# Summing the experts' gated output in DRAM with adding DMAs from GpSimd's queue

## Chip, cores and metric

The kernel runs on one core of one Trainium2 chip. The metric is the device time of one launch in microseconds. The time before is the median of three runs, and the trace is one execution of the same program taken by the hardware profiler.

## What is computed

Three stages follow each other: a linear attention with a normalization, a feed-forward net with a leaky activation (2048 hidden columns), and a mixture of eight experts over 2304 tokens of 512 columns. The change lies in the last stage. Cut to it, the reference is:

```python
for e in range(E):                          # E = 8, w1[e] is 512 x 1024, w2[e] is 1024 x 512
    h = np.maximum(x @ w1[e], 0.0)
    ye = h @ w2[e]
    out += P[:, e:e + 1] * ye               # P: gates, tokens x experts
```

The inputs and the output are float32; `P` comes from a fixed number of row and column scalings of the exponentials of `x @ w_gate`.

## The kernel before

All products are made from halves: each float32 operand is split into two float16 parts, and three matmuls (high by high, high by low, low by high) are summed in PSUM. On top of that, both layers of an expert use a Strassen-like scheme with seven products (numbered 0 to 6) for a 2 x 2 block product. The net counts as layers e = 0 and 1 (`M` = 2), the experts as e = 2 to 9 (`NL` = 10). So "the third expert" is e = `M + 2` = 4.

The tokens are worked on in three parts p (`NP` = 3). For each expert and part there are four units of the first layer (`Quad`, matmuls of 384 columns) and then three units of the second layer (`Outs`, o = 0 to 2, matmuls of 256 columns): 9 output units for each expert. An output unit makes a 2 x 128 x 512 block of the output: two token tiles b and two column halves d, four parts c11, c12, c22 and c21. It has three chains of products on banks of PSUM:

- `chain_a` sums products 0, 5, 6 and 3 in one bank. After each of the first three, ScalarE copies the partial sum u out (`take_u`) before the next product is added. The last state is the part c21.
- `chain_c` makes product 4; VectorE adds u and has c22; product 2 is added in the same bank, and with u it is c12.
- `chain_d` makes product 1; with u it is c11.

Each of c11, c12 and c22 is then added, multiplied by the gate of its token, to a sum buffer in SBUF (`add_to`); c21 goes there directly from PSUM. There are two sum buffers (`acc`), used in turn, so unit n uses the buffer of unit n - 2. Before the adds, SP loads the sums of the former experts from `accd` in DRAM (`acc_load`); after them it stores the buffer to `accd` (`end`, `store`). The first expert (e = 2) leaves its bare product there, the second multiplies it by the first gate. The last expert stores each part to the result `out` as soon as it is there, 128 KB at a time.

What sets the order: all instructions of all engines are put in line by a planner (`Sched`) before the launch. It runs the program as a model several times, derives a latest start of each step from the run before, and always takes the step with the earliest start and then the least due time. A step with several ways (a list) is given to the engine that is free first. Each engine and each DMA queue then runs its list strictly in order. SP's queue carries the weights, the inputs x (`x_load`), and the traffic of `accd`; GpSimd's queue carries three small loads at the start. Nearly all instructions outside the matmuls are issued through one helper and show as line L164; matmuls of the products show as L403.

Of the kernel before, what the change touches and what calls it, by code (L numbers as in the profile page):

```python
# [15 lines left out]
AF = mybir.ActivationFunctionType  # L16
# [242 lines left out]
def fused_kernel(ctx: ExitStack, tc: tile.TileContext, qT, k, v, g_norm, w_in, w_out, alpha,  # L259
# [7 lines left out]
    nc = tc.nc  # L267
# [35 lines left out]
    def program(sc):  # L303
# [712 lines left out]
        def acc_load(n):  # L1016
            e, p, o = outs[n]
            if n >= 2:
                yield acc_left[outs[n - 2]]
            if e > M:  # L1020
                yield acc_left[e - 1, p, o]
                yield from dma(P * D * 8, (acc[n % 2], accd[p * TPB + o].rearrange("p (b d) -> p b d", b=2)))
            acc_ready[e, p, o].set()
# [19 lines left out]
        class Unit:  # L1043


            def __init__(self, n, turn, raw):
                self.n, self.turn, self.held, self.raw = n, turn, 2, raw
                self.buf = [raw[:, q, :] for q in range(4)]
                self.u, self.c22 = [ev() for _ in range(3)], ev()
# [231 lines left out]
        class Outs(Unit):  # L1281
# [38 lines left out]
            def end(self, b, d):  # L1320
                acc_done[self.e].set()
                self.adds -= 1
                if self.e == NL - 1:
                    t, sl = self.ts[b], slice(d * 256, (d + 1) * 256)
                    sc.add(self.store(P * D * 2, out[t * P:(t + 1) * P, sl], self.acc(b, d)))
                elif self.adds == 0:
                    sc.add(self.store(P * D * 8, accd[self.p * TPB + self.o].rearrange("p (b d) -> p b d", b=2), self.sums))

            def store(self, nbytes, dst, src):
                yield from dma(nbytes, (dst, src))  # L1330
# [31 lines left out]
            def take_c21(self, ps):  # L1362
# [5 lines left out]
                self.give(ps)  # L1368
                self.end(1, 0)

        seats = Slots(sc, range(3))

        def layers():

            todo, late, slot, users = [], [], 0, {}
            for k_, (e, p) in enumerate(order):
                net = e < M
                keys = [(b, f) for b in range(2) for f in range(8)] if net else \
                    [(m_, i) for i in range(4) for m_ in range(7)]
                for key in keys:  # L1380
                    hop_done[(e, p), *key], hop_used[(e, p), *key] = ev(), ev(DC if net else TPB)
                    hop[(e, p), *key] = hops[slot]
                    hop_free[(e, p), *key] = users[slot] if slot in users else \
                        kv_done[2 if slot < 13 else 3] if slot < 26 else spread_done
                    users[slot] = hop_used[(e, p), *key]
                    slot = (slot + 1) % len(hops)
                split = len(late) if not net else len(late) // 2 if k_ in (1, NP) else 0
                todo += late[:split] + [(Quad, e, p, i) for i in range(4)] + late[split:]
                late = [(Ys, e, p, b, o) for b in range(2) for o in range(DC)] if net else []
                if not net:  # L1390
                    todo += [(Outs, e, p, o) for o in range(TPB)]
            for n, (kind, e, p, *x) in enumerate(todo):
                if kind == Ys:
                    seat = yield from seats.get()
                    Ys(n, seat, e, p, *x).start()
                    continue
                turn = yield from flight.get()
                if kind == Quad:
                    yield xb_ready[e][p]
                    if e < M:  # L1400
                        yield const_ready
                raw = yield from unit_bufs.get()
                kind(n, turn, raw, e, p, *x).start()
# [135 lines left out]
```

## Time and profile before

| | |
|---|---|
| median of three runs | 1807.35 us |
| lowest, highest | 1801.12 us, 1809.96 us |
| profiled execution, first to last instruction | 1807.8 us |
| TensorE, VectorE, ScalarE busy | 1770.8 us, 1438.4 us, 1156.5 us |
| GpSimd busy | 5.9 us |
| moved by DMA | 195.16 MB |

The span of the profiled execution is the only time that its page gives. The busy times are averages over stages with different limits, so a stage is read from its own stretch, and what ends a wait there. A granted clock of 1.00 is 2.4 GHz, 0.50 would be 1.2 GHz.

### The profile page before, as it was taken

Reading aid. Unit: us, or ns where it says so; the run is one execution under the profiler, and the core shown is the slowest. Engines: PE = TensorE matmul, PEld = TensorE weight load, DVE = VectorE, ACT = ScalarE, POOL = GpSimd, SP = SyncE. Lnnn points to the kernel's source line nnn. Section 1 sums busy time; section 2 is a strip of 40 time slices with the busy share of each in tenths; the row PEclk is TensorE's granted clock in tenths of the full one; section 3 lists DMA queues with packets and bytes.
Section 4 is the critical chain, followed back from the end, with each engine's and each line's share of the span. In section 5 each row is a group of like instructions: output and inputs, shape, how many; then the busy total and the mean of one; then the engine's idle time right before and its main releaser. Section 6 shows DMA issues by size and latency. Waiting matters only on the chain.

```text
span 1807.8 us, 32280 instructions
## 1 busy us (share of the span) xinstructions
PE 1770.8 (98%) x12898; PEld 1277.1 (71%) x12898; DVE 1438.4 (80%) x3158; ACT 1156.5 (64%) x2463; POOL 5.9 (0%) x15
## 2 busy tenths in 40 slices
PE   4999999999999999999999999999999999999999
PEld 3765666666677767777777777777777777777777
DVE  4789976668777999899868878886998688788666
ACT  5767864636586777667746666764677576566443
POOL 1000000000000000000000000000000000000000
PEclk9789999999999999999999999999999999999999
DMA  9532221302032042513423331343224234212231
GB/s 307 176 108 106 68 71 62 108 1 108 1 143 85 24 155 94 189 53 138 161 88 117 144 123 43 130 166 127 80 108 174 71 117 148 104 36 101 102 132 47
DMA packets 52598, 195.16 MB, mean 108 GB/s; under 512 B 4944, under 2 KB 12640, under 8 KB 49760
## 3 DMA queue, kind: packets, MB, share of 16 engines
q1 hardware_dynamic: 52304, 193.09, 30.1%
q8 instruction: 100, 1.64, 0.4%
q14 instruction: 50, 0.41, 0.1%
q0 software_dynamic: 144, 0.03, 0.0%
HBM read 141.58 MB, written 51.51 MB: 107 GB/s over the span
## 4 chain that ended last, share of the span: by engine, by line
PE 93%; DVE 3%; ACT 2%; DMA 1%; issue 0%; SPq 0%; ACTq 0%
PE ps L403 89%; DVE arena L164 3%; ACT arena L164 2%; PE ps L450 2%; DMA arena<-in_v_dram 1%; PE ps L164 1%; PE ps L531 1%; PE ps L541 1%; DMA arena<-in_w_in_dram 0%; PE ps L712 0%; SPq L164 0%; PE ps L501 0%; ACT L164 0%; ACTq L164 0%
## 5 line engine op out<-in xcount | busy, mean ns | idle before, releaser
L403 PE MATMUL ps<-arena 128*128 128x256 f16 (+1 forms) x12240 | 1678.8, 300 | 7.4 <-DVE arena L164 3.8
L403 PEld LDWEIGHTS <-arena 128*128 128x128 f16 x12240 | 1196.8, 98 | 477.7 <-issue 12.4
L164 ACT ACTIVATE arena<-arena 128x384 f16<-128x384 f32 (+6 forms) x1577 | 871.4, 598 | 238.9 <-DVE arena L164 186.9
L164 DVE TENSOR_TENSOR arena<-arena 128x384 f16<-128x384 f32 (+7 forms) x1566 | 826.2, 572 | 53.1 <-ACT arena L164 47.3
L164 ACT ACTIVATE arena<-ps 128x384 f32<-128x384 f32 (+3 forms) x691 | 306.4, 452 | 352.7 <-PE ps L403 331.2
L164 DVE SCALAR_TENSOR_TENSOR arena<-arena 128x384 f32<-128x384 f32 (+3 forms) x558 | 308.5, 562 | 36.2 <-DMA arena<-accd 17.1
L164 DVE SCALAR_TENSOR_TENSOR arena<-ps,arena 128x384 f32<-128x384 f32 (+1 forms) x423 | 233.7, 555 | 79.0 <-PE ps L403 63.7
L164 DVE TENSOR_TENSOR arena<-ps,arena 128x256 f32<-128x256 f32 x216 | 90.7, 425 | 97.5 <-ACT arena L164 58.6
L164 ACT ACTIVATE arena<-ps,arena 128x384 f32<-128x384 f32 x96 | 55.4, 580 | 52.1 <-PE ps L403 50.8
L450 PE MATMUL ps<-arena 128*128 128x128 f32 (+1 forms) x160 | 37.8, 402 | 24.4 <-DMA arena<-in_v_dram 24.4
L450 PEld LDWEIGHTS ps<-arena 128*128 128x128 f32 (+1 forms) x160 | 31.6, 284 | 29.2 <-issue 28.4
L164 DVE TENSOR_SCALAR arena<-arena 128x1 int32<-128x1 int32 (+8 forms) x198 | 45.0, 242 | 8.8 <-ACT arena L164 6.7
L164 DVE SCALAR_TENSOR_TENSOR arena<-arena,ps 128x384 f32<-128x384 f32 x24 | 14.4, 613 | 28.9 <-PE ps L403 28.7
L164 DVE TENSOR_REDUCE arena<-ps 128x1 f32<-128x128 f32 x26 | 7.5, 287 | 30.9 <-PE ps L164 30.8
L164 DVE TENSOR_REDUCE arena<-arena 128x1 f32<-128x384 f32 (+7 forms) x66 | 22.5, 349 | 6.4 <-ACT arena L164 5.9
L541 PEld LDWEIGHTS ps<-arena 128*128 128x128 f32 x144 | 20.9, 219 | 4.8 <-issue 2.5
L531 PE MATMUL ps<-arena 128*128 128x384 f32 (+1 forms) x64 | 22.6, 496 | 0.0
L541 PE MATMUL ps<-arena 128*128 128x2 f32 x144 | 21.3, 270 | 0.9 <-ACT arena L164 0.9
L164 PE MATMUL ps<-arena 128*128 128x128 f32 (+2 forms) x92 | 21.2, 303 | 0.5 <-ACT arena L164 0.5
L164 ACT ACTIVATION_READ_ACCUMULATOR arena<-arena 128x1 f32 x96 | 18.5, 193 | 0.0
L164 DVE TENSOR_TENSOR arena<-arena,ps 128x384 f32<-128x384 f32 x24 | 12.7, 549 | 6.6 <-PE ps L164 6.3
L531 PEld LDWEIGHTS ps<-arena 128*128 128x128 f32 x64 | 13.2, 232 | 3.8 <-issue 2.2
(25 smaller groups left out, 50.8 us busy)
## 6 DMA issues: line engine op xcount, KB each, us to landing
arena<-xd SPq DMA_DIRECT2D x16, 2688.0 KB, 9.6
arena<-in_w_dram SPq DMA_DIRECT2D x64, 512.0 KB, 4.5
accd<-arena SPq DMA_DIRECT2D x63, 512.0 KB, 2.9
arena<-accd SPq DMA_DIRECT2D x63, 512.0 KB, 3.7
xd<-arena SPq DMA_DIRECT2D x5, 2688.0 KB, 9.7
arena<-in_w_in_dram SPq DMA_DIRECT2D x16, 512.0 KB, 5.2
arena<-in_w_out_dram SPq DMA_DIRECT2D x16, 512.0 KB, 4.5
arena<-in_qT_dram SPq DMA_DIRECT2D x6, 768.0 KB, 7.9
```

The costliest lines, as they stand in the source:

```text
L164: way[2](*way[3], **way[4])
L403: r = nc.tensor.matmul(ps[:, 0:ncols], x, y, start=(start and i == 0 and m == 0), stop=(stop and i == n - 1 and m == 2), skip_group_check= ...
L450: nc.tensor.matmul(ps[:, sl], kt[0:n, c, sl], vt[0:n, c, sl], start=(c == 0), stop=(c == 4))
L531: nc.tensor.matmul(ps[:, r0:r1], kvbd[b][:, c, :], qs[j][:, c, r0:r1], start=True, stop=True)
L541: nc.tensor.matmul(sums[:, o * H + 2 * c:o * H + 2 * c + 2], sq[:, o * P:(o + 1) * P], heads, start=True, stop=True)
```

## The change

For the experts e = 4 to 9 a new class, `Adds`, takes the place of `Outs`. Every part leaves PSUM multiplied by the gate, the three u as well as c11, c12, c22 and c21 before anything is added to them. Each of the seven drains can go to ScalarE or VectorE. The adding is left to DMA, into `out` itself: u0 and u1 (both column halves of the first tile, 256 KB) and u2 (one half of the second tile, 128 KB) by `store_first`, then the whole sum buffer (512 KB) by `store_last`, which waits until the first two have landed. These DMAs have the accumulate operation and are issued on GpSimd's queue. The sum buffers are still two, used in turn; they are no longer loaded, and a buffer is free again when the 512 KB add of its unit has landed. The second expert (e = 3) stores its sums to `out` in place of `accd`, and only it loads from `accd`.

```diff
@@ -1017,7 +1017,7 @@
             e, p, o = outs[n]
             if n >= 2:
                 yield acc_left[outs[n - 2]]
-            if e > M:
+            if e == M + 1:
                 yield acc_left[e - 1, p, o]
                 yield from dma(P * D * 8, (acc[n % 2], accd[p * TPB + o].rearrange("p (b d) -> p b d", b=2)))
             acc_ready[e, p, o].set()
@@ -1320,11 +1320,11 @@
             def end(self, b, d):
                 acc_done[self.e].set()
                 self.adds -= 1
-                if self.e == NL - 1:
-                    t, sl = self.ts[b], slice(d * 256, (d + 1) * 256)
-                    sc.add(self.store(P * D * 2, out[t * P:(t + 1) * P, sl], self.acc(b, d)))
-                elif self.adds == 0:
-                    sc.add(self.store(P * D * 8, accd[self.p * TPB + self.o].rearrange("p (b d) -> p b d", b=2), self.sums))
+                if self.adds == 0:
+                    dst = accd[self.p * TPB + self.o].rearrange("p (b d) -> p b d", b=2)
+                    if self.e > M:
+                        dst = out.rearrange("(j o p) d -> o p j d", o=TPB, p=P)[self.o][:, 2 * self.p:2 * self.p + 2, :]
+                    sc.add(self.store(P * D * 8, dst, self.sums))
 
             def store(self, nbytes, dst, src):
                 yield from dma(nbytes, (dst, src))
@@ -1367,6 +1367,71 @@
                     yield from self.add_to(1, 0, ps[:, 0:256])
                 self.give(ps)
                 self.end(1, 0)
+
+        class Adds(Outs):
+
+
+            def __init__(self, n, turn, raw, e, p, o):
+                super().__init__(n, turn, raw, e, p, o)
+                self.flat = raw.rearrange("p q n -> p (q n)")
+                self.left, self.first, self.last_, self.added = 2, ev(3), ev(4), ev()
+                self.dst = out.rearrange("(j o p) d -> o p j d", o=TPB, p=P)[o][:, 2 * p:2 * p + 2, :]
+
+            def start(self):
+                super().start()
+                sc.add(self.store_first())
+                sc.add(self.store_last())
+
+            def gated(self, dst, ps, b):
+                col = pcols[self.e % 3][:, self.ts[b]:self.ts[b] + 1]
+                return [A(256, nc.scalar.activation, dst, ps[:, 0:256], AF.Copy, scale=col),
+                        V(256, nc.vector.tensor_scalar, dst, ps[:, 0:256], col, None, op0=mult)]
+
+            def take_u(self, ps, n):
+                yield pcol_done[self.e]
+                yield self.gated(self.flat[:, n * 256:(n + 1) * 256], ps, n // 2)
+                self.u[n].set()
+                self.first.set()
+
+            def take(self, ps, b, d, after):
+                yield pcol_done[self.e]
+                yield acc_ready[self.e, self.p, self.o]
+                yield self.gated(self.acc(b, d), ps, b)
+                after()
+                acc_done[self.e].set()
+                self.last_.set()
+
+            def take_c11(self, ps):
+                return self.take(ps, 0, 0, lambda: banks.put(ps))
+
+            def take_c12(self, ps):
+                return self.take(ps, 0, 1, lambda: self.give(ps))
+
+            def take_c22(self, ps):
+                return self.take(ps, 1, 1, self.c22.set)
+
+            def take_c21(self, ps):
+                return self.take(ps, 1, 0, lambda: self.give(ps))
+
+            def add(self, nbytes, *parts):
+                for dst, src in parts:
+                    yield "G", 1.0, nc.gpsimd.dma_start, (dst, src), {"accum_op": add}
+                sc.dma_free = max(sc.dma_free, sc.now + 0.65) + nbytes / 180e3
+                yield sc.dma_free + 1.5
+
+            def store_first(self):
+                yield self.first
+                x = self.flat[:, 0:768]
+                yield from self.add(P * 256 * 12, (self.dst[:, 0, :], x[:, 0:512]), (self.dst[:, 1, 256:512], x[:, 512:768]))
+                self.added.set()
+                self.release()
+
+            def store_last(self):
+                yield self.last_
+                yield self.added
+                yield from self.add(P * D * 8, (self.dst, self.sums))
+                acc_left[self.e, self.p, self.o].set()
+                self.release()
 
         seats = Slots(sc, range(3))
 
@@ -1388,7 +1453,7 @@
                 todo += late[:split] + [(Quad, e, p, i) for i in range(4)] + late[split:]
                 late = [(Ys, e, p, b, o) for b in range(2) for o in range(DC)] if net else []
                 if not net:
-                    todo += [(Outs, e, p, o) for o in range(TPB)]
+                    todo += [(Outs if e < M + 2 else Adds, e, p, o) for o in range(TPB)]
             for n, (kind, e, p, *x) in enumerate(todo):
                 if kind == Ys:
                     seat = yield from seats.get()
```

The planner puts the whole program in line anew. GpSimd's queue, its last rows before (`arena` is SBUF, `in_...` are inputs):

```order
L1430 MEMSET arena 64x1
L1431 MEMSET arena 128x2048 [waits Pool_49]
L1433 DMA arena<-in_g_norm_dram 64x1 x2
L1434 DMA arena<-in_alpha_dram 128x16x1
L1435 DMA arena<-in_w_gate_dram 128x4x8
L1535 UNCONDITIONAL_BRANCH
L1535 ISA [waits barrier_Pool_Activation_PE_DVE_SP_gather]
```

and after, the rows of the three output units of the second part of e = 5; `out_dram` is the result, 128x512 is the DMA of u0 and u1, 128x256 that of u2, 128x2x512 that of the sum buffer; DMASW are the semaphores of DMAs from this queue:

```order
L164 DMA out_dram<-arena 128x512 [waits DVE_49,Activation_49]
L164 DMA out_dram<-arena 128x256 [waits Activation_49]
L164 DMA out_dram<-arena 128x512 [waits DVE_49,Activation_49]
L164 DMA out_dram<-arena 128x256 [waits DMASW3_49,Activation_49]
L164 DMA out_dram<-arena 128x2x512 [waits DMASW4_49,DMASW1_49,DMASW0_49]
L164 DMA out_dram<-arena 128x2x512 [waits DMASW3_49,DMASW2_49,Activation_49]
L164 DMA out_dram<-arena 128x512 [waits DVE_49,Activation_49]
L164 DMA out_dram<-arena 128x256 [waits DMASW7_49,DVE_49]
```

Where the queue ended with the start-up loads, 162 adding DMAs now stand. The two first units' 512 KB adds stand behind the small adds of the second unit and wait for DMAs of the same queue, and the third unit's small adds stand behind them.

VectorE in an output unit of e = 5 before; `ps` are banks of PSUM, DMAHW are semaphores of DMAs from SP's queue:

```order
L164 TENSOR_TENSOR arena<-ps_64,arena 128x256 [waits PE_49]
L164 SCALAR_TENSOR_TENSOR arena<-arena 128x256 [waits DMAHW1_49,DVE_49]
L164 TENSOR_TENSOR arena<-ps_66,arena 128x256 [waits Activation_49]
L164 SCALAR_TENSOR_TENSOR arena<-arena 128x256 [waits DVE_49]
L164 SCALAR_TENSOR_TENSOR arena<-ps_68,arena 128x256 [waits PE_49]
L164 TENSOR_TENSOR arena<-ps_66,arena 128x256 [waits PE_49]
```

and VectorE after, at the third of the three units named above and into the first-layer units behind it:

```order
L164 TENSOR_SCALAR arena<-ps_65,arena 128x256 [waits PE_49]
L164 TENSOR_SCALAR arena<-ps_66,arena 128x256 [waits DMASW4_49,Activation_49]
L164 TENSOR_SCALAR arena<-ps_67,arena 128x256 [waits PE_49,Activation_49]
L164 SCALAR_TENSOR_TENSOR arena<-ps_68,arena 128x384 [waits Activation_49]
L164 SCALAR_TENSOR_TENSOR arena<-ps_70,arena 128x384 [waits PE_49]
L164 SCALAR_TENSOR_TENSOR arena<-ps_68,arena 128x384 [waits PE_49]
```

and ScalarE after, at the same third unit:

```order
L164 ACTIVATE arena<-ps_65,arena 128x256 [waits PE_49]
L164 ACTIVATE arena<-ps_69 128x384 [waits DVE_49,PE_49]
L164 ACTIVATE arena<-ps_67,arena 128x256 [waits DMASW4_49,Activation_49]
L164 ACTIVATE arena<-ps_69 128x384 [waits PE_49]
L164 ACTIVATE arena<-ps_65,arena 128x256 [waits PE_49,Activation_49]
L164 ACTIVATE arena<-ps_69 128x384 [waits PE_49]
```

The sums out of PSUM and the gated adds are gone; one gated drain each stands for them, on either engine. The first drain of each engine that writes the sum buffer again waits for a semaphore of GpSimd's DMAs (DMASW4), and the drains of the first-layer units (128x384) stand behind it.

## Rows read from the trace of the kernel before

**Rows 1.** The page: busy time of each engine, and the chain's shares by engine.

```profile
PE 1770.8 (98%) x12898; PEld 1277.1 (71%) x12898; DVE 1438.4 (80%) x3158; ACT 1156.5 (64%) x2463; POOL 5.9 (0%) x15
...
PE 93%; DVE 3%; ACT 2%; DMA 1%; issue 0%; SPq 0%; ACTq 0%
```

**Rows 2.** Busy time in stretches: start:end, length, engines busy (instructions), clock, DMA share, GB/s.

```profile
40.00:145.00 105.00, 103.64 (x536) 72.31 (x535) 82.46 (x213) 75.96 (x171) 0.00 (x0) 0.82 0.42 139
520.00:780.00 260.00, 253.90 (x2018) 188.35 (x2016) 225.76 (x550) 188.82 (x399) 0.00 (x0) 1.00 0.30 113
780.00:845.00 65.00, 64.45 (x493) 48.02 (x492) 60.57 (x136) 49.67 (x106) 0.00 (x0) 1.00 0.27 92
880.00:1700.00 820.00, 819.71 (x6289) 615.51 (x6288) 655.90 (x1392) 521.16 (x1130) 0.00 (x0) 1.00 0.31 111
1205.00:1370.00 165.00, 165.00 (x1267) 123.85 (x1266) 134.39 (x282) 108.38 (x236) 0.00 (x0) 1.00 0.31 111
```

**Rows 3.** The chain in order of time: start, length, what, instructions.

```profile
510.30 7.20 PE ps L403 x66
...
590.80 12.69 PE ps L403 x78
...
824.95 12.96 ACT arena L164 x27
...
1531.09 269.49 PE ps L403 x2064
```

**Rows 4.** The timeline of the last 8 us: start, length, engine, what, [idle before].

```profile
1801.04 2.91 PE L403 MATMUL ps<-arena 128*128 128x256 f16 x24 [0.47 <-ACT arena L164]
...
1804.51 0.48 DVE L164 SCALAR_TENSOR_TENSOR arena<-arena 128x256 f32<-128x256 f32 x1
```

**Rows 5.** Groups by shape: count, busy us, mean ns, idle before.

```profile
L164 ACT ACTIVATE arena<-ps 128x384 f32<-128x384 f32 x456 | 219.5, 488 | 140.9 <-PE ps L403 131.8 <-PE ps L531 5.2 <-PE ps L541 1.7
...
L164 DVE TENSOR_TENSOR arena<-ps,arena 128x256 f32<-128x256 f32 x216 | 90.7, 425 | 97.5 <-ACT arena L164 58.6 <-PE ps L403 37.8
L164 DVE SCALAR_TENSOR_TENSOR arena<-arena 128x256 f32<-128x256 f32 x189 | 89.5, 485 | 19.5 <-DMA arena<-accd 17.1 <-DMA out_dram<-arena 0.3
L164 ACT ACTIVATE arena<-ps 128x256 f32<-128x256 f32 x225 | 84.4, 381 | 200.5 <-PE ps L403 199.4
...
L164 ACT ACTIVATE arena<-ps,arena 128x384 f32<-128x384 f32 x96 | 55.4, 580 | 52.1 <-PE ps L403 50.8 <-DVE arena L164 0.4
...
L164 DVE SCALAR_TENSOR_TENSOR arena<-ps,arena 128x256 f32<-128x256 f32 x63 | 30.6, 485 | 35.0 <-PE ps L403 35.0
...
L164 DVE TENSOR_SCALAR arena<-arena 128x256 f32<-128x256 f32 x36 | 12.0, 354 | 0.4 <-DMA arena<-accd 0.3
```

**Rows 6.** SP's own waits: total us, times, longest.

```profile
SPq L164 <- DVE arena L164: 1135.1, 148, 64.0
```

**Rows 7.** Waits of the engines: total us, times, longest.

```profile
DVE arena L164 <- DMA arena<-accd: 17.4, 11, 3.7
```

**Rows 8.** GpSimd's timeline at the start: its DMA instructions.

```profile
4.67 1.19 POOL L1434 DMA_DIRECT2D arena<-in_alpha_dram  x1
5.85 0.77 POOL L1435 DMA_DIRECT2D arena<-in_w_gate_dram  x1
```

**Rows 9.** DMA issues: instructions, KB each, median us from issue to landing.

```profile
arena<-xd SPq DMA_DIRECT2D x16, 2688.0 KB, 9.6
...
accd<-arena SPq DMA_DIRECT2D x63, 512.0 KB, 2.9
arena<-accd SPq DMA_DIRECT2D x63, 512.0 KB, 3.7
...
out_dram<-arena SPq DMA_DIRECT2D x36, 128.0 KB, 1.8
...
arena<-in_g_norm_dram POOLq DMA_DIRECT2D x2, 0.2 KB, 6.0
arena<-in_alpha_dram POOLq DMA_DIRECT2D x1, 8.0 KB, 8.8
```

## The prediction, made before the changed kernel ran

> **What bounds the kernel now.** I read the shares first. TensorE is busy for 98% of the span, VectorE 80%, ScalarE 64%, GpSimd for nothing after the start [rows 1]. A share is no proof that TensorE has nothing to give, so I went to the stretches. From 880 us to 1700 us, five expert lengths, TensorE is busy for all but 0.3 of 820 us at a granted clock of 1.00 (2.4 GHz) [rows 2]. The chain of waits, in order of time, has one piece of 269.49 us with 2064 matmuls without a break, up to 1800.6 us [rows 3]. The last question is whether the matmuls inside are at their own pace. 66 matmuls of 256 columns take 7.20 us, 109 ns each, and 78 of 384 columns take 12.69 us, 163 ns each [rows 3]. One expert has 504 of the wide and 756 of the narrow kind: 504 x 0.163 + 756 x 0.109 = 164.6 us, and a stretch of 165 us holds 1267 matmuls [rows 2]. So TensorE's own rate is the bound wherever the changed units run, and drains and DMA lie beside it.
>
> The Trainium skill, "TensorE: Matmul & The Clock Gate", section on 56 against 53.3 ns, gives 2.5 ns over columns divided by 2.4 GHz for a matmul in a dense run. The trace agrees (109 ns for 256 columns). By it an expert cannot take under 164.3 us, which speaks against any gain from faster drains.
>
> Where TensorE does wait is earlier: 6.1 us in 520 to 780, 0.55 us in 780 to 845 [rows 2]. The six changed experts end with the last matmul at 1803.95 us [rows 4]; at 165 us each they begin near 814 us. TensorE's idle time that the changed units could win back is therefore about 1 us: 0.29 us in the steady stretch, the 0.55 us at 780 to 845 and the 0.47 us before the last 24 matmuls [rows 2, 4].
>
> **The change, part by part.** Each expert has 9 output units, so 54 units change, in 18 groups of three; 0.109 us is the price of a narrow matmul throughout.
>
> Arithmetic. Away go, per unit, three sums out of PSUM (0.425 us), three gated adds (0.485 us) and one gated add out of PSUM (0.485 us) on VectorE, 3.2 us, and three copies of 0.381 us on ScalarE [rows 5]. For 54 units that is 173 us of VectorE and 62 us of ScalarE. Seven gated drains per unit come in, 378; the order puts 299 on ScalarE and 79 on VectorE. No row has one. On ScalarE, a 384-column drain costs 0.488 us plain and 0.580 us with a scale column [rows 5], so I take 0.381 + 0.092 = 0.47 us; on VectorE 0.42 us, between the 0.354 us tensor_scalar in SBUF and the 0.425 us sum from PSUM. ScalarE gains 299 x 0.47 - 62 = 79 us, VectorE loses 173 - 79 x 0.42 = 140 us; in an expert's 165 us ScalarE goes from 108 to 121 us and VectorE from 134 to 111 [rows 2]. Neither becomes the bound, and TensorE does not run faster for it. Price: 0.
>
> SP. 54 loads and 54 stores of accd (9 of these come back as stores to the result) and the 36 small stores of the result go. SP now stands for 1135 us waiting for VectorE [rows 6], mostly in stores, with the weight and x loads behind; those loads can now start earlier. VectorE's 17.4 us of waits for accd [rows 7] shrink too. The chain is 93% TensorE and 1% DMA [rows 1]; from 825 to 838 us it runs through ScalarE [rows 3], before the first changed drains (814 us plus four first-layer units of 27 us in all), and after that nearly always through TensorE. Price: 0.
>
> GpSimd's adds. This is the unknown. Each unit issues three adding DMAs (256 KB, 128 KB, then 512 KB), and the last waits for the other two. No row shows an adding DMA. Issue: two that GpSimd does issue take 1.19 and 0.77 us of its time [rows 8]; I take 0.77 us. Landing L of 512 KB: from below, a plain store of that size, 2.9 us; from above, the slowest DMA from GpSimd's queue, 8.8 us, which ran while the start-up loads filled the engines [rows 9]. Between: stores of 128 and 512 KB land in 1.8 and 2.9 us, so 1.4 us plus 0.37 us per 128 KB; loads of 512 and 2688 KB in 3.7 and 9.6 us, so 2.3 us plus 1.4 us per 512 KB. An add must read the destination and the source before it writes. A load and a store end to end give 3.7 + 2.9 = 6.6 us; both reads pipelined, one fixed part of 2.5 us (my choice, a load's 2.3 and a little) plus 2 x 1.4 us, give 5.3 us. I take 5.3 us, since in every row bytes stream through the engines rather than in phases; the first pair then takes L1 = 3.9 us. The ends stay 2.9 (L1 2.2) and 8.8 us (L1 6.0, as the g_norm loads) [rows 9].
>
> The Trainium skill, "DMA: Bandwidth & Descriptors", section on the GpSimd path, gives 2.0 us plus bytes over 436 GB/s; "Collectives: The Full Stack", section on the bandwidth ceiling, says an add in the DMA engine halves the rate because it reads two sources. Together an estimate of 4.4 us (L1 3.2). No run here shows it; by it the sum below would be 1.6 us lower and the verdict the same.
>
> Who waits for an add: a sum buffer is used again two units later, so only the third unit of a group follows closely; before the next group stand four first-layer units, 168 wide matmuls, 27 us. The third unit's first gated drain waits for the first unit's 512 KB add, and in the queues of ScalarE or VectorE everything behind it waits as well. I counted matmuls in the new order from the one that feeds the first unit's third u part to the first that needs the third unit's drained part: 130 to 152 in 17 groups, 14.7 to 18.1 us at the two prices (the last group has no such matmul). What has to fit: drain 0.47 + two issues 1.54 + L1 3.9 + issue 0.77 + L 5.3 + drain 0.47 = 12.5 us. It fits in all, with 2 us over in the tightest. End to end (L1 5.1, L 6.6) it is 15.0 us: over in one group, by 0.3 us. At the upper end it is 18.1 us: over in 16 of 17, 25 us in all. **Price taken: 0; bounds 0 and 25 us.** Other transfers can stretch an add: an x load of 2688 KB, 9.6 us [rows 9], starts as each group begins. The margin of 2 us covers that only in part; I put 1 us for a few collisions.
>
> End. Now the last matmul ends at 1803.95 us, two VectorE steps and a 128 KB store follow, and the span ends at 1807.8 us (the table of times): 3.85 us [rows 4, 9]. In the new order the last unit's third u part is fed 18 matmuls, 2.0 us, before the end; then 0.47 + 1.54 + 3.9 + 0.77 + 5.3 = 12.0 us, so the end is 10.0 us after the last matmul: **+6.1 us**. With the lower bound +2.0, end to end +8.6, with the upper +11.7 us.
>
> Before the third expert. Nothing is added there, but the planner orders the whole program by one set of due times, and the order already differs in the first 45 matmul rows. In those stretches TensorE waits 1.4 us (40 to 145 us) and those 6.1 us [rows 2]; I allow 3 us either way and take 0.
>
> Sum: 6 + 1 + 0 = +7 us on the profiled 1807.8 us, 1814.8 us; that span lies 0.45 us above the median of the three runs, so 1814 us, 0.4% over the median.
>
> **The rivals.** First, the adds land too late and hold the drains of the third unit: a wait for a DMA in place of one for arithmetic. Against it: 2 us of margin at the value taken. For it: no row shows an adding DMA, and all of GpSimd's landed slowly. It decides once L1 + L passes about 11.5 us; at the upper end +25 and +11.7 give 1844 us, and each further us of L + L1 costs about 17 us. Slower; 0.25. Second, the relief of VectorE and SP pays: the waits of 520 to 845 us go with the new order, 6.6 us, and the adds land as fast as stores, +2 us: 1803 us. For it: those waits are put down to VectorE and ScalarE; against it: no unit before 814 us loses an instruction. 0.08. Third, the planner's new order before 814 us is itself worse by up to 6 us: 1820 us; 0.10. That the change does not do what it says I give nothing: the new order shows all 162 adds and all 378 gated drains.
>
> **How the numbers follow.** The forecast, hidden adds and a longer end, has 0.57: 1809 to 1817 us. The measurement tells about 0.5% from no change, 9 us: 1798.3 to 1816.4 us. Of the forecast's 0.57 about 0.13 lies above (L over 6.5 us); with the first rival's 0.22 and the third's 0.07 slower has 0.42. Faster by over 0.5% needs more than all waits of TensorE after 500 us: 0.02. Same: 0.56. The range 1802 to 1842 us reaches to the second rival and most of the first; at most 0.2 lie beyond.
>
> **What would show it.** Right: TensorE still busy for 165 of 165 us in the steady stretches, ScalarE near 121 and VectorE near 111 us there; 512 KB adds that land in 4 to 7 us; no waits of ScalarE or VectorE for an adding DMA that reach TensorE; some 10 us between the last matmul and the end. Wrong: TensorE idle before narrow matmuls once per group, ended by ScalarE or VectorE and behind them a DMA to the output; adds over 8 us; or a difference that is there before 814 us.

## The result and the profile after

The changed kernel takes 1819.52 us (median of 20 runs, 1812.04 to 1826.62) and the kernel before 1808.19 us (20 runs). The ratio is **1.0066, 95% interval 1.0053 to 1.0080**: slower by 12 us (9.6 to 14.5). The 20 runs of either kernel fall into 7 shorter and 13 longer ones, and the changed kernel is 11.5 us slower among the shorter and 12.1 us among the longer, so the 12 us are not a matter of the mix. The profiled execution has a span of 1818.2 us, 10.4 us over that of before.

The page, busy time of each engine and the last chain's shares by engine; these answer to [rows 1]:

```profile
PE 1770.1 (97%) x12898; PEld 1274.8 (70%) x12898; DVE 1324.0 (73%) x2859; ACT 1227.3 (67%) x2600; POOL 166.2 (9%) x177
...
PE 83%; DVE 8%; ACT 4%; DMA 3%; issue 1%; SPq 0%; POOLq 0%; ACTq 0%
```

VectorE has 114 us less to do and ScalarE 71 us more, and TensorE's busy time is what it was. The time went elsewhere. The same stretches as in [rows 2] (start:end, length, busy time and instructions of TensorE, its weight loads, VectorE, ScalarE and GpSimd, then clock, DMA share, GB/s):

```profile
40.00:145.00 105.00, 103.99 (x542) 72.43 (x541) 81.36 (x209) 76.89 (x174) 0.00 (x0) 0.82 0.44 145
520.00:780.00 260.00, 252.25 (x1994) 187.06 (x1993) 223.49 (x542) 187.19 (x395) 0.00 (x0) 0.99 0.31 112
780.00:845.00 65.00, 64.72 (x488) 47.58 (x486) 59.90 (x134) 49.53 (x108) 0.00 (x0) 1.00 0.21 70
880.00:1700.00 820.00, 818.41 (x6268) 613.22 (x6266) 565.17 (x1151) 580.11 (x1241) 132.39 (x135) 1.00 0.51 104
1205.00:1370.00 165.00, 164.49 (x1259) 122.94 (x1257) 116.54 (x237) 120.58 (x257) 26.73 (x27) 1.00 0.51 110
```

In 880 to 1700 us TensorE is idle for 1.6 us, against 0.3 us before; in 520 to 780 for 7.8 us, against 6.1 us. The end is the largest single piece. The timeline of the last 15 us (start, length, engine, what, [idle before]):

```profile
1804.29 4.16 PE L403 MATMUL ps<-arena 128*128 128x256 f16 x36 [0.23 <-ACT arena L164]
...
1804.54 0.90 POOL L164 DMA_DIRECT2D out_dram<-arena  x1 [3.45 <-ACT arena L164]
1806.45 0.47 ACT L164 ACTIVATE arena<-ps,arena 128x256 f32<-128x256 f32 x1 [1.85 <-PE ps L403]
...
1807.22 0.86 POOL L164 DMA_DIRECT2D out_dram<-arena  x1 [1.78 <-ACT arena L164]
1808.55 0.47 ACT L164 ACTIVATE arena<-ps,arena 128x256 f32<-128x256 f32 x1 [0.90 <-PE ps L403]
1810.70 1.20 POOL L164 DMA_DIRECT2D out_dram<-arena  x1 [2.62 <-DMA out_dram<-arena]
```

The last matmul ends at 1804.29 + 4.16 = 1808.45 us and the last drain at 1809.02 us. GpSimd then sits until 1810.70 us, waiting for the small add that it issued at 1807.22 us, and only then issues the last 512 KB. The span ends at 1818.2 us, **9.75 us after the last matmul; before it was 3.85 us** [rows 4].

The adding DMAs and the plain ones beside them (issues, KB each, median us from the start of the issue to the landing; [rows 9]):

```profile
out_dram<-arena POOLq DMA_DIRECT2D x54, 512.0 KB, 6.2
out_dram<-arena POOLq DMA_DIRECT2D x54, 256.0 KB, 4.5
...
out_dram<-arena POOLq DMA_DIRECT2D x54, 128.0 KB, 3.2
...
accd<-arena SPq DMA_DIRECT2D x9, 512.0 KB, 2.6
```

The groups by shape that came in (count, busy us, mean ns, idle before and what ended it; [rows 5]): the adds' issue on GpSimd, and the gated drains on ScalarE and VectorE.

```profile
L164 POOL DMA_DIRECT2D out_dram<-arena x162 | 160.3, 1052 | 1644.9 <-DVE arena L164 1044.2 <-ACT arena L164 537.5 <-DMA out_dram<-arena 33.9
...
L164 ACT ACTIVATE arena<-ps,arena 128x256 f32<-128x256 f32 x299 | 134.3, 472 | 160.8 <-PE ps L403 154.0 <-DMA out_dram<-arena 5.2
...
L164 DVE TENSOR_SCALAR arena<-ps,arena 128x256 f32<-128x256 f32 x79 | 37.2, 481 | 178.5 <-PE ps L403 157.4 <-DMA out_dram<-arena 20.5
```

The waits (total us, times, longest): the drains do wait for adding DMAs, 11 times and 25.7 us in all, up to 8.3 us at once; TensorE's own waits for the two engines, before the matmuls of line L403, are 10.0 us in all.

```profile
POOL out_dram L164 <- DMA out_dram<-arena: 33.9, 13, 5.7
...
DVE arena L164 <- DMA out_dram<-arena: 20.5, 7, 8.3
...
PE ps L403 <- ACT arena L164: 5.7, 9, 1.7
...
ACT arena L164 <- DMA out_dram<-arena: 5.2, 4, 3.2
PE ps L403 <- DVE arena L164: 4.3, 5, 2.6
```

### The profile page after: what moved, and what is told of

It reads as the page before. It is cut to its first block, busy times and chain, and to the rows that moved or that the text cites. A ratio compares the mean times of both kernels' runs of the same rounds, so it can differ in the third digit from the quotient of the medians.

```text
span 1818.2 us, 32451 instructions
## 1 busy us (share of the span) xinstructions
PE 1770.1 (97%) x12898; PEld 1274.8 (70%) x12898; DVE 1324.0 (73%) x2859; ACT 1227.3 (67%) x2600; POOL 166.2 (9%) x177
## 4 chain that ended last, share of the span: by engine, by line
PE 83%; DVE 8%; ACT 4%; DMA 3%; issue 1%; SPq 0%; POOLq 0%; ACTq 0%
PE ps L403 80%; DVE arena L164 8%; ACT arena L164 4%; PE ps L450 1%; DMA arena<-in_v_dram 1%; DMA arena<-in_w_dram 1%; PE ps L531 1%; PE ps L164 1%; PE ps L541 1%; DMA arena<-in_w_in_dram 1%; SPq L164 0%; DMA arena<-accd 0%; DMA out_dram<-arena 0%; PE ps L712 0%; PE ps L501 0%
## 5 line engine op out<-in xcount | busy, mean ns | idle before, releaser
L403 PE MATMUL ps<-arena 128*128 128x384 f16 (+1 forms) x12240 | 1681.2, 300 | 10.4 <-ACT arena L164 5.7
L403 PEld LDWEIGHTS <-arena 128*128 128x128 f16 x12240 | 1197.3, 98 | 483.7 <-issue 16.2
L164 ACT ACTIVATE arena<-ps 128x384 f32<-128x384 f32 (+3 forms) x529 | 247.3, 475 | 158.5 <-PE ps L403 137.0
L164 ACT ACTIVATE arena<-ps,arena 128x256 f32<-128x256 f32 (+1 forms) x395 | 189.9, 498 | 214.8 <-PE ps L403 206.8
L164 POOL DMA_DIRECT2D out_dram<-arena x162 | 160.3, 1052 | 1644.9 <-DVE arena L164 1044.2
L164 DVE SCALAR_TENSOR_TENSOR arena<-ps,arena 128x384 f32<-128x384 f32 (+1 forms) x369 | 206.9, 564 | 84.0 <-PE ps L403 57.4
L164 DVE SCALAR_TENSOR_TENSOR arena<-arena 128x384 f32<-128x384 f32 (+3 forms) x396 | 231.1, 591 | 16.5 <-ACT arena L164 13.6
L164 DVE TENSOR_SCALAR arena<-ps,arena 128x256 f32<-128x256 f32 (+1 forms) x82 | 38.2, 475 | 179.8 <-PE ps L403 157.4
L164 DVE TENSOR_TENSOR arena<-ps,arena 128x256 f32<-128x256 f32 x54 | 22.6, 420 | 14.8 <-PE ps L403 11.3
L164 DVE TENSOR_REDUCE arena<-arena 128x1 f32<-128x384 f32 (+7 forms) x66 | 22.4, 349 | 10.5 <-ACT arena L164 9.8
L541 PEld LDWEIGHTS ps<-arena 128*128 128x128 f32 x144 | 20.4, 214 | 4.5 <-issue 2.2
```

The lines of the kernel that those rows point to most:

```text
L164: way[2](*way[3], **way[4])
L403: r = nc.tensor.matmul(ps[:, 0:ncols], x, y, start=(start and i == 0 and m == 0), stop=(stop and i == n - 1 and m == 2), skip_group_check= ...
L541: nc.tensor.matmul(sums[:, o * H + 2 * c:o * H + 2 * c + 2], sq[:, o * P:(o + 1) * P], heads, start=True, stop=True)
```

## How the kernels below are compared

Executions of one and the same kernel differ by up to 19 us (before, 35 runs of one series: 1798.72 to 1817.60 us). Part of that lies in the start: from 40 to 145 us the granted clock was 0.76 to 0.89 in the profiles of this case, where later stretches, up to the last matmul, have 0.97 to 1.00. A span of a single profile therefore proves little, and each kernel below is judged by its ratio to runs of before on the same chip. Its profile gives two things that the start doesn't touch: the **end**, from the last matmul to the end of the span, and TensorE's **idle** time from 145 us to the last matmul. Against before (end 3.85 us, idle 6.64 us up to 845 us and 0.76 us after) they make a sum that can be set beside the ratio:

| kernel | end | idle 145 to 845 | idle 845 to last matmul | sum over before | ratio, as us of 1808 | ratio [95%] |
|---|---|---|---|---|---|---|
| changed | 9.75 | 8.0 | 2.3 | +8.9 | +11.9 | 1.0066 [1.0053, 1.008] |
| 1 no adds | 1.47 | 8.5 | 1.4 | +0.1 | +3.4 | 1.0019 [0.9998, 1.004] |
| 2 plain copies | 6.3 | 8.8 | 2.6 | +6.5 | +8.0 | 1.0044 [1.0019, 1.007] |
| 3 one more copy | 13.5 | 7.9 | 11.4 | +21.6 | +22.2 | 1.0123 [1.0089, 1.0156] |
| 4 two more copies | 18.1 | 8.5 | 51.8 | +67.1 | +88 | 1.0487 [1.0455, 1.052] |
| 5 last expert as before | 4.0 | 8.5 | 5.5 | +6.8 | +5.4 | 1.003 [1.0006, 1.0054] |
| 6 last expert only | 10.6 | 7.7 | 2.2 | +9.2 | +11.6 | 1.0064 [1.0039, 1.009] |
| 7 before, order 0.39 | 3.9 | 7.9 | 1.2 | +1.8 | +0.9 | 1.0005 [0.998, 1.003] |
| 8 before, order 0.41 | 3.9 | 8.0 | 2.2 | +2.9 | +1.4 | 1.0008 [0.9984, 1.0032] |
| 9 changed, order 0.39 | 9.4 | 11.3 | 3.2 | +12.6 | +13.6 | 1.0075 [1.005, 1.0101] |
| 10 changed, order 0.41 | 9.8 | 11.6 | 3.2 | +13.4 | +15.0 | 1.0083 [1.0056, 1.011] |

Kernel 4 apart, the sum stands within 3.4 us of the measured loss everywhere, which is within every interval but that of the changed kernel, where it falls 0.7 us short of the lower end. So the two terms are most of the account, and the experiments say what each is made of. Two cautions go with the columns of idle time. The changed kernel and kernels 1 to 4 have one order, and from 145 to 845 us they show 7.9 to 8.8 us, so a difference under 1 us between two profiles shows nothing. And profiles differ in how far they are at 845 us, so a wait near it can fall on either side; the two columns together are safer than each. (In kernel 4 the granted clock after 845 us is 0.98 as well; 2% of its 1024 us there is 20 us, which is about what the sum lacks.) Kernel 4 from 845 us to its last matmul:

```profile
845.00:1869.16 1024.16, 972.39 (x7319) 723.34 (x7316) 638.53 (x1302) 660.53 (x1417) 216.63 (x265) 0.98 0.61 149
```

## Experiments

**Theory:** the loss is the longer end, some 6 us, and little else; the adds fit behind the matmuls. **First rival:** the adds hold the drains of the third unit of each group. **Second rival:** the planner's new order is what costs.

### Kernels 1 and 2: no adds, and copies in place of adds

Both keep the changed kernel's order on every engine.

```diff
-                    yield "G", 1.0, nc.gpsimd.dma_start, (dst, src), {"accum_op": add}
+                    yield "G", 1.0, lambda *a: None, (dst, src), {}                  # kernel 1
+                    yield "G", 1.0, nc.gpsimd.dma_start, (dst, src), {}              # kernel 2
```

> The changed kernel with every instruction of every engine in the same order, but without its 162 adding DMAs (the output then lacks the experts from the third on). Theory end (the loss is mainly the two adds in series after the last matmul): no DMA waits, last matmul some 2 to 3 us earlier than in the changed kernel, span ending within 1 us of the last drain, so about 9 us less behind the last matmul; time 1807 to 1810 us against 1819.5, ratio to the kernel before 0.999 to 1.001. Theory order (the planner's new order costs the time before the third expert): time over 1812 us, since the order is untouched. Theory hold (the adds hold the drains of the third units): as theory end, but the last matmul 5 us or more earlier than in the changed kernel.

> The changed kernel with the same order, its 162 DMAs as plain copies from the same queue in place of adds (the output is then the last product written, not the sum). It prices the adding by itself. If adding reads two sources and so takes longer, 512 KB land in 4 to 5 us against 6.2, the two in series at the end save 2 to 3.5 us, and the waits of the third units shrink: time 1815 to 1817.5 us, ratio 1.004 to 1.005. If the landing is set by GpSimd's queue and not by the adding: 512 KB still near 6 us, time as the changed kernel, ratio 1.0066.

Kernel 1's last timeline rows:

```profile
1793.17 4.16 PE L403 MATMUL ps<-arena 128*128 128x256 f16 x36 [0.23 <-ACT arena L164]
...
1797.43 0.47 ACT L164 ACTIVATE arena<-ps,arena 128x256 f32<-128x256 f32 x1 [0.90 <-PE ps L403]
```

The last drain ends the program, 1.47 us after the last matmul. The ratio falls from 1.0066 to 1.0019, by 8.5 us; the end is shorter by 9.75 - 1.47 = 8.3 us. One wait of TensorE, 0.78 us, falls just behind 845 us in the changed kernel and ahead of it in kernel 1:

```profile
845.50 1.25 PE L403 MATMUL ps<-arena 128*128 128x256 f16 x10 [0.78 <-ACT arena L164]
```

```profile
835.27 0.93 PE L403 MATMUL ps<-arena 128*128 128x256 f16 x7 [0.78 <-ACT arena L164]
```

Over both columns TensorE's idle time falls from 10.4 to 9.9 us, where before has 7.4 us. So nearly everything that the adds cost in this order is the end. By what was expected it is a miss all the same: 1812.62 us lies over the 1807 to 1810 us of the theory of the end and just over the 1812 us of the theory of the order, and 1.0019 lies over 0.999 to 1.001, though its interval reaches into that range. What stays, 1.0019, is not the adds', and by itself it isn't shown, as the interval reaches 1. Kernel 1's end is 2.4 us shorter than that of before and its idle time 2.5 us longer, so by the profile the new order and the new drains, which kernel 1 keeps, cost what the shorter end gains. Its last matmul comes 11.1 us earlier than in the changed kernel, but 10.2 of these are there at the wait shown, before any add: they come from the start of the program and not from held drains.

Kernel 2's DMAs from the same queue, same tiles, same semaphores, without the adding:

```profile
out_dram<-arena POOLq DMA_DIRECT2D x54, 512.0 KB, 3.2
out_dram<-arena POOLq DMA_DIRECT2D x54, 256.0 KB, 2.6
...
out_dram<-arena POOLq DMA_DIRECT2D x54, 128.0 KB, 2.0
```

6.2, 4.5 and 3.2 us with the adding stand against 3.2, 2.6 and 2.0 us without (expected for 512 KB were 4 to 5 us): from 128 to 512 KB an add grows by 3.0 us and a copy by 1.2 us, 2.5 times. GpSimd's issue is shorter too (in 880 to 1700 us 80.82 us for 134 DMAs, 0.60 us each, against 132.39 us for 135, 0.98 us). The end is 6.3 us, 3.5 us shorter, and the ratio 4 us lower; no wait of VectorE or ScalarE for a DMA to the result is left.

### Kernels 3 and 4: hold the sum buffer longer

Behind each 512 KB add GpSimd issues one plain copy of the sum buffer to a scratch tile (kernel 4: two), so the buffer comes free later; order otherwise as in the changed kernel.

```diff
+                def add_and_copy(dst, src):
+                    nc.gpsimd.dma_start(dst, src, accum_op=add)
+                    for _ in range(1 if src is self.sums else 0):      # kernel 4: 2
+                        nc.gpsimd.dma_start(scratch, src)
-                    yield "G", 1.0, nc.gpsimd.dma_start, (dst, src), {"accum_op": add}
+                    yield "G", 1.0, add_and_copy, (dst, src), {}
```

> The changed kernel with the same order, and behind each 512 KB add a plain 512 KB copy of the same sum buffer from the same queue to a scratch place in DRAM. The buffer is free when both have landed. Theory hold with the counted margins (14.7 to 18.1 us from the third u part to the matmul in need; chain now 0.47 + 2.1 + 4.5 + 1.05 + 6.2 + 0.47 = 14.8 us): about 1 us of issue and half a microsecond of sharing more, chain near 16 us, some 3 to 6 us in all over the 17 groups, and 1 to 2 us at the end: 1823 to 1828 us, ratio 1.008 to 1.011. If the adds had a wide margin: the end alone, 1821 us, ratio 1.0075. If the adds already held each group: 17 x 1.5 = 25 us more.

> As the run with one more copy, with two: the second waits for the first, since both write the same scratch place, so the buffer comes free about 5 us later. Theory hold with the counted margins: chain near 20 us, (20 - 16.6) us in each of 17 groups, 50 to 65 us in all, time 1870 to 1890 us, ratio 1.035 to 1.045; waits of ScalarE and VectorE for DMAs of GpSimd's queue once per group, and behind them idle time of TensorE. If the sum buffers were not the place: the time grows by the end alone, 5 to 7 us, 1826 us.

The waits of kernel 3, then those of kernel 4:

```profile
DVE arena L164 <- DMA accd<-arena: 66.8, 12, 15.7
...
PE ps L403 <- ACT arena L164: 14.3, 15, 2.3
ACT arena L164 <- DMA accd<-arena: 13.9, 6, 6.3
```

```profile
DVE arena L164 <- DMA accd<-arena: 158.6, 17, 20.4
ACT arena L164 <- DMA accd<-arena: 62.4, 15, 10.0
PE ps L403 <- ACT arena L164: 44.1, 21, 5.5
PE ps L403 <- DVE arena L164: 15.2, 9, 3.1
```

With one copy more, the drains wait in 18 places instead of 11, and TensorE's idle time after 845 us goes from 2.3 to 11.4 us; with two it goes to 51.8 us. The waits named are for the extra copies (`accd` is the scratch tile), which also lengthen GpSimd's issue and the traffic. The mechanism of the first rival is thus real, it has its place where the prediction put it, and it is steep. In the changed kernel it stands just short of its point: the drains wait already, TensorE hardly. Kernel 3's ratio, 1.0123, lies over what was expected of counted margins, but 3.8 us of it are its own longer end; kernel 4's, 1.0487, lies over 1.045.

### Kernels 5 and 6: adds everywhere but in the last expert, and only there

```diff
-                    todo += [(Outs if e < M + 2 else Adds, e, p, o) for o in range(TPB)]
+                    todo += [(Adds if M + 2 <= e < NL - 1 else Outs, e, p, o) for o in range(TPB)]   # kernel 5
+                    todo += [(Outs if e < NL - 1 else Adds, e, p, o) for o in range(TPB)]            # kernel 6
                     ...
```

In kernel 5 the last expert loads its sums from the result, as `Outs` did from `accd`, and stores its parts 128 KB at a time; in kernel 6 the experts before the last are made as before and e = 8 stores to the result. Both are planned anew.

> Experts e = 4 to 8 keep the adding DMAs; the last expert, e = 9, is made as in the kernel before (sums loaded, now from the result, added by VectorE, stored in parts of 128 KB). The planner orders the whole program anew. Theory that half of the loss is the longer end (9.75 us after the last matmul against 3.85 us): the end falls back to 3.5 to 5 us, ratio to before 1.001 to 1.005, what is left being the order's own share. Rival, that adding in DRAM holds the drains throughout: 45 of 54 units still do it, ratio 1.005 to 1.007, with waits of ScalarE and VectorE for DMAs to the result that reach TensorE.

> Only the last expert, e = 9, leaves its adding to DMAs; e = 3 to 8 load and store sums as before, and e = 8 stores its sums to the result. The planner orders the whole program anew. Theory of the longer end: the span ends 9 to 10.5 us after the last matmul, ratio to before 1.0033 (6 us) by this alone, with 3 us of order either way 1.0015 to 1.005. Rival, holds throughout: 9 of 54 units, ratio under 1.0015.

The last rows of kernel 5, then of kernel 6:

```profile
1813.42 2.91 PE L403 MATMUL ps<-arena 128*128 128x256 f16 x24 [0.47 <-ACT arena L164]
...
1816.90 0.48 DVE L164 SCALAR_TENSOR_TENSOR arena<-arena 128x256 f32<-128x256 f32 x1
```

```profile
1799.85 3.62 PE L403 MATMUL ps<-arena 128*128 128x256 f16 x31
...
1805.71 1.20 POOL L164 DMA_DIRECT2D out_dram<-arena  x1 [2.94 <-DMA out_dram<-arena]
```

Kernel 5 ends its span at 1820.3 us, 4.0 us after the last matmul; kernel 6 at 1814.1 us, 10.6 us after. Five experts of adds without the last cost 1.0030, one expert of adds at the end costs 1.0064, as much as all six. A cost that were paid in every unit would have it the other way round. That kernel 6 lies above its expected 1.005, with an end of 10.6 us just over the 10.5 us expected, may be the order's share (idle +2.4 us); another 2.4 us no stretch shows. Kernel 5 has 5.5 us idle after 845 us, more than any other kernel without extra copies. But 2.8 us of it are two waits of TensorE for ScalarE that lie ahead of its first add:

```profile
846.70 4.40 PE L403 MATMUL ps<-arena 128*128 128x384 f16 x33 [1.66 <-ACT arena L164]
852.29 2.89 PE L403 MATMUL ps<-arena 128*128 128x256 f16 x25 [1.19 <-ACT arena L164]
...
858.18 0.92 POOL L164 DMA_DIRECT2D out_dram<-arena  x1 [851.49 <-ACT arena L164]
```

So these two are not the adds' doing. Whether the adds have a part in the remaining 2.7 us (0.8 us in the kernel before) isn't shown.

### Kernels 7 to 10: the same instructions in another order

One constant of the planner is moved by 0.01, in the kernel before (7, 8) and in the changed kernel (9, 10).

```diff
-MIX = 0.4
+MIX = 0.39      # kernels 7 and 9
+MIX = 0.41      # kernels 8 and 10
```

> The kernel before with one planner constant changed (MIX 0.4 to 0.39): the same instructions, another order, no adding DMAs. Theory that a new order alone costs or gives several us: ratio away from 1 by 0.001 to 0.004, seen as TensorE's idle time between 145 and 880 us (before 6.6 us). Rival, the order is worth nothing: within 0.0007 of 1, idle time within 1 us.

> The kernel before with the same constant moved the other way (0.4 to 0.41); the order differs from TensorE's 45th row on. As for 0.39: a new order alone gives a ratio away from 1 by 0.001 to 0.004 by the one theory, within 0.0007 by the other.

> The changed kernel with the planner constant at 0.39 in place of 0.4: the same instructions in another order. Theory that the loss is the longer end (6 us) plus the waits that any new order brings (2 to 3 us of TensorE idle between 145 and 880 us) plus what the start of the program costs in this order: the end again 9.5 to 11 us after the last matmul, ratio 1.004 to 1.008. Rival, that half of the loss was bad luck of the one order: ratio 1.0035 or less, in this order or in that of 0.41.

> The changed kernel with the constant at 0.41. As for 0.39: ratio 1.004 to 1.008 with an end of 9.5 to 11 us by the one theory, 1.0035 or less by the other.

TensorE before the first changed unit, 145 to 845 us, in the kernel before, the changed one, kernel 7, kernel 8, kernel 9 and kernel 10 (columns as above; one fence each):

```profile
145.00:845.00 700.00, 693.36 (x4936) 470.07 (x4935) 576.67 (x1287) 465.19 (x962) 0.00 (x0) 1.00 0.24 87
```

```profile
145.00:845.00 700.00, 691.97 (x4912) 468.77 (x4910) 574.22 (x1281) 461.25 (x957) 0.00 (x0) 1.00 0.24 85
```

```profile
145.00:845.00 700.00, 692.06 (x4949) 471.40 (x4948) 573.84 (x1281) 465.09 (x963) 0.00 (x0) 1.00 0.25 90
```

```profile
145.00:845.00 700.00, 692.03 (x4916) 469.03 (x4914) 570.05 (x1280) 460.56 (x957) 0.00 (x0) 1.00 0.24 86
```

```profile
145.00:845.00 700.00, 688.75 (x4889) 466.51 (x4887) 570.20 (x1272) 458.30 (x950) 0.00 (x0) 1.00 0.23 84
```

```profile
145.00:845.00 700.00, 688.38 (x4898) 467.33 (x4897) 567.50 (x1269) 458.68 (x952) 0.00 (x0) 1.00 0.24 88
```

Eight orders of this program were profiled, counting kernels 5 and 6: 6.6 us idle in this stretch in the one of before, 7.7 to 8.8 us in five others, 11.3 and 11.6 us in the last two. The order of before waits least, and any other waits 1 to 5 us longer, without an instruction being added here. For the kernel before, that is too little for its ratio (1.0005 and 1.0008, and both intervals contain 1), so between the theories of kernels 7 and 8 the runs don't decide; the idle time was above the 1 us of the rival. For the changed kernel they do decide: in two other orders it is slower again, 1.0075 and 1.0083, with both intervals wholly above 1.0035 and ends of 9.4 and 9.8 us; the idle time ahead of the changed units grew by nearly 5 us, more than the 2 to 3 us expected. The loss is not bad luck of one order.

## Why the prediction was right, and where it was short

The time lies in the range, 5.5 us over the 1814 us forecast, and the mechanism is the one taken: hidden adds, a longer end. But the loss is over 0.5%, the case to which the prediction gave 0.42 and not the 0.56 of no change. By its steps:

- **TensorE is the bound, relief of VectorE and SP is worth nothing: right.** 1770.8 us busy before, 1770.1 after; VectorE 134 to 117 us and ScalarE 108 to 121 us of 165 (predicted 111 and 121). The prediction's least time of an expert, 164.3 us, should read 164.4 us, which changes nothing. VectorE's gated drain took 0.481 us, not 0.42; ScalarE's 0.472, as taken. SP waits 967.3 us for VectorE in place of 1135.1 [rows 6], and nothing came of it.

```profile
SPq L164 <- DVE arena L164: 967.3, 86, 69.3
```

- **The end, +6.1 us: right in sum, by two errors that cancel, which is luck.** Measured +5.9. From the start of the third u part's drain (1806.45 us) to the 512 KB add's issue 5.9 us were predicted, 4.25 us passed: the add of u0 and u1 was out at 1804.54 us, so one small add stood in the way and not two. From there to the end 6.1 us were predicted, 7.5 us passed. The add itself took what was taken for its issue and landing together, 0.77 + 5.3 us; it landed 6.1 us after its issue began (the view of the last add below). The other 1.4 us lie between the landing and the end of the program. The prediction's sum stops at the landing, while the 3.85 us of before, from which it is subtracted, hold such a piece: the last store, issued at 1805.0 us, landed 1.7 us later, 1.1 us before the end. Kernel 1 shows that this term is nearly the adds' whole price, and kernels 5 and 6 agree.

```profile
DMA to landing us min/median/max: 6.1/6.1/6.1
```

- **Landing, 5.3 and 3.9 us taken, with 0.77 us for each issue on top: right in sum, not as counted.** The medians of 6.2 and 4.5 us begin with the issue and hold it. The end shows this: the last small add is issued at 1807.22 us for 0.86 us, and the add that waits for it starts at 1810.70 us, 3.5 us after the issue's start and 2.6 us after its end, where the median of that size is 3.2 us. So 0.77 + 5.3 = 6.1 us and 0.77 + 3.9 = 4.7 us are what to set against 6.2 and 4.5 us; GpSimd's issue alone was longer, 1.05 us. Whether the two reads are pipelined, as taken, isn't shown by this. The estimate of 4.4 us that the prediction drew from the Trainium skill ("DMA: Bandwidth & Descriptors", section on the GpSimd path, with "Collectives: The Full Stack", section on the bandwidth ceiling) is further off. The plain DMAs of kernel 2 agree with the first page's 2.0 us plus bytes over 436 GB/s at 512 and 256 KB (3.2 and 2.6 us), but 128 KB took 2.0 us and not 2.3, and the adding cost 2.5 times per byte and not twice.
- **The hold of the third unit, price 0 and 1 us for collisions: right in the price, with less room than thought.** The chain that had to fit, from the third u part's drain of the first unit through its 512 KB add to one more drain, was summed to 12.5 us. In the trace of the changed kernel it takes 11.0 to 16.2 us in the 17 groups, median 14.3, against the counted gaps of 14.7 to 18.1 us. The small adds took less than summed: in every group the 128 KB add was the later of the two to land, so one of them stood in the way and not both. The last link took more: the first unit's 512 KB adds, which run beside other transfers, landed after 5.9 to 11.1 us, median 7.7, and the third units', with no other add under way, after 5.6 to 6.2 us. What stretches the first ones, other adds or loads, isn't shown. So the drains wait (11 times), and yet TensorE loses about 0.5 us by the adds (10.4 us idle after 145 us, 9.9 us in kernel 1), which is within the scatter. Kernels 3 and 4 show what lies behind the edge. The longest of the 17 chains runs from the second of the two drains in the first row, on ScalarE, to the drain on VectorE that waits for the add:

```profile
1021.33 0.84 ACT L164 ACTIVATE arena<-ps,arena 128x256 f32<-128x256 f32 x2 [1.06 <-PE ps L403]
...
1037.42 0.88 DVE L164 TENSOR_SCALAR arena<-ps,arena 128x256 f32<-128x256 f32 x2 [0.82 <-DMA out_dram<-arena]
```

- **The order before the third expert, 3 us either way and 0 taken: this is the short step.** Kernel 1, without any add, has 2.5 us more idle time than before (9.9 against 7.4 us); with the adds' 0.5 us and the end's 5.9 us that makes the +8.9 us. The third rival, a worse order for up to 6 us, is therefore part of what happened, on top of the forecast and not in place of it: 2.5 us by the idle time, up to 5.5 us if the 3 us below are the order's as well; kernels 9 and 10 pay nearly 5 us there. A new order should have had a positive price, since before's order waits less than any other that was profiled.
- **What is left:** the profiled pair differs by 10.4 us, 1.5 us more than the sum, the ratio by 11.9 us (9.6 to 14.5). The sum is also short of the ratio in kernels 1 and 6, by 3.3 and 2.4 us, and over it in kernels 5, 7 and 8, by 0.9 to 1.5 us. Whether the changed order also costs something in the first 145 us, where one profile per kernel says little, stays open.

The second rival (the relief pays) is refuted: VectorE had 114 us less to do, but the waits between 145 and 845 us that it was to win back went from 6.6 to 8.0 us, and a 512 KB add took 6.2 us where a store took 2.9 us. No version tried is faster than the kernel before.

## What to carry to other kernels

Here TensorE had next to no idle time; moving additions from VectorE into adding DMAs bought nothing, and the last unit paid for their serial chain in full. On such a kernel, cost the end first, from the last matmul to the last landing and from there to the end of the program, and keep the last expert's output on the path with the short tail. Where a buffer is freed by an adding DMA, set its whole chain (drain, issues, both landings, with the landings as they are beside other DMAs) against the gap of the next user, and don't add the issue to a landing time that already holds it; take the chain seriously when less than a few microseconds are over. Where a planner reorders everything, price the new order above zero if the old one waits little.

## What the runs showed of the hardware

- An adding DMA from SBUF to DRAM on GpSimd's queue took 6.2, 4.5 and 3.2 us for 512, 256 and 128 KB, the same DMAs without the adding 3.2, 2.6 and 2.0 us: about 131 against 328 GB/s per further byte (384 KB in 3.0 and 1.2 us). These are medians; 512 KB adds took 5.6 to 6.2 us in the third units and 5.9 to 11.1 us in the first, beside other transfers. GpSimd spent 0.98 us against 0.60 us on issuing one.
- The granted clock was below 1.00 on average in two kinds of stretch, between its two levels of 1.00 (2.4 GHz) and 0.50 (1.2 GHz). In the changed kernel's last 10.2 us, with TensorE busy for 0.45 us, it is 0.64; in kernel 4, whose TensorE waited 51.8 us after 845 us, it is 0.98 there. But from 40 to 145 us of the changed kernel it is 0.82 with TensorE busy for 103.99 of 105 us, and in the 40 us before that 0.96 with TensorE busy for 13.04 us, so idle time alone does not account for it. The end of the changed kernel as a stretch, columns as above:

```profile
1808.00:1818.20 10.20, 0.45 (x5) 0.15 (x2) 0.00 (x0) 0.47 (x1) 1.28 (x2) 0.64 0.48 66
```
